# One float32 key tile becomes 16-bit for every even head, and the experts' inner values of two blocks go through one instruction with x requested four blocks ahead

## The chip, the cores and the metric

The kernel runs on one core of a Trainium2 chip. The metric is the device time in microseconds, the median of several executions. The core has five engines that run their own instruction streams and wait for one another through semaphores: TensorE (PE in the rows, with its weight loads as PEld), VectorE (DVE), ScalarE (ACT), GpSimd (POOL) and SyncE (SP), which here only issues DMAs. Matmuls write to PSUM, the other operands lie in SBUF.

## What is computed

The output of a pooled attention is the input of a routed mixture of experts (cut from the reference):

```python
# attention: q, k, v are (4, 8, 1152, 64)
q_pool = q.reshape(B, H, S // 2, 2, D).mean(axis=3)            # 576 queries per head
scores = (1.0 / np.sqrt(D)) * np.matmul(q_pool, k.transpose(0, 1, 3, 2))
attn = np.exp(scores - scores.max(-1)); attn /= attn.sum(-1) + 1e-09
x = np.matmul(attn, v)                                          # -> (4, 576, 512)
# experts: w_gate (512, 8), w_local (512, 1), w1 (8, 512, 1024), w2 (8, 1024, 512)
logits = x @ w_gate
local_gate = sigmoid(x @ w_local)
for b, s:                                                       # token by token
    fresh = argmax(logits[b, s])
    e = fresh if s == 0 or local_gate[b, s] < 0.5 else prev_e
    out[b, s] = softmax(logits[b, s])[e] * (relu(x[b, s] @ w1[e]) @ w2[e])
```

## The kernel before

**Attention** goes over 32 heads, two of which (heads n = 2p and 2p + 1, j = n % 2) are a pair p. A head has nine tiles of 128 keys, so there are 288 steps s, with n, kt = divmod(s, 9). A step emits the score matmuls of its key tile (`scores`: lines 223 and 225) and the exp of the result on ScalarE (line 227, into `PHI`, float32), one or two units that find row maxima for the head after (`max_unit`: matmuls of lines 189, 195 and 197 into one of two PSUM tiles, and a reduction on VectorE, lines 190 and 199), and, six steps late (`LAG`), the products with V (`av`). For the precision of V the kernel has two ways. A tile kt in `F32K = (4, 8)` takes float32 operands: five matmuls on `PHI` and `VX` (line 261). All other tiles take 16-bit parts: the upper half of the float32 number as bfloat16 (`top`), the rest as float16 in `PLO`, V as `VT` with a high and a low part, three matmuls (lines 263 to 265) for each of five query tiles. The rest in `PLO` is a subtraction of 576 columns (`low`, line 237), for an even step on GpSimd and for an odd one on VectorE; two steps share one call, after the exp of both. `prep_ops(p)` turns the loaded K, Q and V of a pair into operands, one op for each step from step 13 of the pair two before: among them `o6` (V to `VT`, line 159 on ScalarE, in two pieces since tile 4 is left out) and `o7` (the low part, line 162 on GpSimd, two pieces in two steps). `extra(s)` loads and splits the experts' first weights: at s = 40 + 14c VectorE runs line 510 once.

**Experts.** Tokens are sorted into 23 blocks of 128 with one expert each. Eight phases ph go over the blocks j, i = 23 ph + j: phases 0 to 3 make 256 inner values each (`mm1`, 24 matmuls of line 1061), phases 4 to 7 make 128 outputs each (`mm2`, line 1069). All engines run their streams in the order written. For a step i the loop in `experts` writes: the copy of block i + 1's weights on VectorE (line 934, three buffers `wc`); the request of x for block i + 3 (`xready`: line 988 stores x in phase 1, line 995 loads it from block 12 of phase 2 on, into six slots that are freed by twos); for the next phase's weights, 16 pieces c, a load (line 491, four buffers `wf`), three steps after it two ScalarE passes (lines 499 and 501), one step after these the low part (line 508 on GpSimd in phases 1 to 3, line 510 on VectorE else); then the block's matmuls, a relu on ScalarE (line 944) and, one step later (`pend`), the low part of the relu on VectorE (line 945). SyncE issues all these DMAs in this order, so a load that waits for its buffer holds the ones behind it.

```python
n = i + 3
if NST <= n < 4 * NST:
    xready(*divmod(n, NST))
...
f = (mm1 if ph < 4 else mm2)(i)
if pend:
    pend()
pend = f
```

Of the kernel before, what the change touches and what calls it, by code (L numbers as in the profile page):

```python
# [8 lines left out]
F32 = mybir.dt.float32  # L9
F16 = mybir.dt.float16  # L10
# [3 lines left out]
AF = mybir.ActivationFunctionType  # L14
# [11 lines left out]
F32K = (4, 8)  # L26
PREP0 = 13
# [5 lines left out]
def attention(tc, psum, stg, kT, qeo, vL, ident, emit_x, extra, load_ident, drain):  # L33
# [15 lines left out]

    VT = [lat.tile([128, 2, NKT - 2, 130], F16, name=f"vt{i}") for i in range(3)]  # L50
# [52 lines left out]
    def prep_ops(p):  # L103
# [145 lines left out]
    def av(s):  # L249
        n, kt = divmod(s, NKT)  # L250
        p, j = divmod(n, 2)
        if kt == 0:
            AV[n] = ps_a.tile([128, 512], F32, name="av", tag="av")
        a = AV[n]
        ph, pl = top(PHI[s // 2 % NPH]), PLO[s // 2 % NPH]
        v, kv = VT[p % 3], kt - (kt > F32K[0])
        for t in range(5):
            o = a[:, t * 65:t * 65 + 65]
            c = (s % 2) * Q + t * 128
            if kt in F32K:  # L260
                T.matmul(o, PHI[s // 2 % NPH][:, c:c + 128], VX[p % 2][:, j, F32K.index(kt)], start=False, stop=(kt == NKT - 1 and t == 4), skip_group_check=True)  # L261
                continue
            T.matmul(o, ph[:, c:c + 128], v[:, j, kv, 0:65], start=(kt == 0 and t == 0), stop=False, skip_group_check=True)  # L263
            T.matmul(o[:, 0:64], ph[:, c:c + 128], v[:, j, kv, 65:129], start=False, stop=False, skip_group_check=True)  # L264
            T.matmul(o, pl[:, c:c + 128], v[:, j, kv, 0:65], start=False, stop=(kt == NKT - 1 and t == 4), skip_group_check=True)  # L265
# [110 lines left out]
NST = 23  # L376
# [52 lines left out]
class Moe:  # L429
# [507 lines left out]
    def mm1(self, i, p):  # L937

        V, A = self.nc.vector, self.nc.scalar
        ph, j = divmod(i, NST)  # L940
        w = self.wcp.pop(i).rearrange("p (s k f) -> p s k f", s=2, k=4)
        x = self.xt.pop((ph, j))
        h, hl = self.hq[ph][:, 0, j], self.hq[ph][:, 1, j]
        return (lambda: self.block1(p, w, x, 0), lambda: self.block1(p, w, x, 1), lambda: A.activation(out=h, in_=p, func=AF.Relu),
                lambda: V.scalar_tensor_tensor(out=hl, in0=p, scalar=0.0, in1=h, op0=ALU.max, op1=ALU.subtract))
# [27 lines left out]
    def experts(self):  # L973
# [4 lines left out]
        nx = [NST + NST % 2]  # L978

# [18 lines left out]
        def mm1(i):  # L998
# [3 lines left out]
            f = self.mm1(i, self.ps.tile([128, 2, 128], F32, name="psh", tag="ps"))  # L1002
            for k in range(3):
                f[k]()
            return f[3]
# [14 lines left out]
        for i in range(NF, NS):  # L1020
# [11 lines left out]
            n = i + 3  # L1032
# [24 lines left out]
    def block1(self, p, w, x, ft):  # L1057
        n = 0
        for kk in range(4):
            for ws, xs_ in ((0, 0), (0, 1), (1, 0)):  # L1060
                self.nc.tensor.matmul(p[:, ft], w[:, ws, kk, ft * 128:ft * 128 + 128], x[:, 2 * kk + xs_], start=(n == 0 and ft == 0),  # L1061
# [184 lines left out]
```

## Time and profile before

| | |
|---|---|
| median of 3 runs (lowest, highest) | 759.37 us (758.96, 760.9) |
| profiled execution | 763.41 us, span of the trace 761.4 us |
| busy: PE, DVE, POOL, ACT | 697.4 us (92%), 620.5 (81%), 503.4 (66%), 477.0 (63%) |
| granted TensorE clock, mean | 0.985 of 2.4 GHz |
| DMA | 122.99 MB, mean 162 GB/s |

Busy time of matmuls is counted to their modelled ends, and they overlap, so the starts of neighbouring instructions tell more of TensorE's pace than its busy time. A wait is idle time of an engine before an instruction, with what ended it; a wait for several things is put down to the one that came last in the profile.

### The profile page before, as it was taken

Reading aid. Unit: us, or ns where it says so; the run is one execution under the profiler, and the core shown is the slowest. Engines: PE = TensorE matmul, PEld = TensorE weight load, DVE = VectorE, ACT = ScalarE, POOL = GpSimd, SP = SyncE. Lnnn points to the kernel's source line nnn. Section 1 sums busy time; section 2 is a strip of 40 time slices with the busy share of each in tenths; the row PEclk is TensorE's granted clock in tenths of the full one; section 3 lists DMA queues with packets and bytes.
Section 4 is the critical chain, followed back from the end, with each engine's and each line's share of the span. In section 5 each row is a group of like instructions: output and inputs, shape, how many; then the busy total and the mean of one; then the engine's idle time right before and its main releaser. Section 6 shows DMA issues by size and latency. Waiting matters only on the chain. (4 is left out here: it accounts for less than half of the span.)

```text
span 761.4 us, 25799 instructions
## 1 busy us (share of the span) xinstructions
PE 697.4 (92%) x10664; PEld 611.1 (80%) x10664; DVE 620.5 (81%) x1098; ACT 477.0 (63%) x971; POOL 503.4 (66%) x456
## 2 busy tenths in 40 slices
PE   3899999999999999889999998888898999999994
PEld 0487788887778877778887887888897889999994
DVE  7778888888888888888888976689889899798851
ACT  2475777677477667567766655686767675565521
POOL 6575687778367767458666435853647567777776
PEclk9999999999899999999999999999999999999998
DMA  7363643586363586354593226696828884474411
GB/s 241 97 180 121 186 119 109 160 212 154 140 187 81 166 192 169 112 174 102 153 202 72 72 31 173 219 308 214 286 93 280 279 288 165 148 230 145 127 40 32
DMA packets 90058, 122.99 MB, mean 162 GB/s; under 512 B 40552, under 2 KB 46828, under 8 KB 89936
## 3 DMA queue, kind: packets, MB, share of 16 engines
q1 hardware_dynamic: 85152, 110.41, 49.8%
q0 software_dynamic: 4784, 10.86, 4.3%
q8 instruction: 87, 1.43, 0.8%
q14 instruction: 35, 0.29, 0.1%
HBM read 79.29 MB, written 16.85 MB: 126 GB/s over the span
## 5 line engine op out<-in xcount | busy, mean ns | idle before, releaser
L227 ACT ACTIVATE ph<-sc 128x576 f32<-128x576 f32 x288 | 187.6, 652 | 118.3 <-PE sc L225 99.8
L199 DVE TENSOR_REDUCE mx<-psm 128x1 f32<-128x512 f32 (+1 forms) x300 | 193.7, 662 | 57.2 <-PE psm L197 54.9
L237 POOL TENSOR_TENSOR pl<-ph 128x576 f16<-128x576 f32 x112 | 150.2, 1342 | 43.5 <-ACT ph L227 43.5
L934 DVE COPY wc<-w 128x2048 f16 x184 | 154.4, 839 | 26.7 <-PE pso L1069 22.6
L1061 PEld LDWEIGHTS <-wc 128*128 128x128 f16 x2208 | 126.1, 98 | 20.8 <-DVE wc L934 12.1
L264 PE MATMUL av<-vt,ph 128*128 128x64 f16 x1120 | 126.9, 196 | 0.0
L263 PE MATMUL av<-vt,ph 128*128 128x65 f16 x1120 | 126.4, 193 | 0.0
L265 PE MATMUL av<-vt,pl 128*128 128x65 f16 x1120 | 126.1, 192 | 0.0
L1069 PE MATMUL pso<-wc,hq 128*128 128x128 f16 x2208 | 123.4, 219 | 0.0
L1069 PEld LDWEIGHTS <-hq 128*128 128x128 f16 x2208 | 123.3, 98 | 0.0
L264 PEld LDWEIGHTS <-ph 128*128 128x128 bf16 x1120 | 104.9, 98 | 20.1 <-issue 0.5
L1073 POOL DMA_INDIRECT out<-ob,sid x92 | 100.6, 1093 | 30.9 <-issue 18.0
L225 PE MATMUL sc<-qa,ks 65*128 65x288 f16 (+1 forms) x576 | 119.9, 290 | 0.3 <-ACT qa L213 0.3
L263 PEld LDWEIGHTS <-ph 128*128 128x128 bf16 x1120 | 106.2, 98 | 17.2 <-issue 9.6
L223 PE MATMUL sc<-qs,ks 128*128 128x288 f16 x576 | 119.7, 290 | 0.2 <-ACT ph L227 0.2
L237 DVE TENSOR_TENSOR pl<-ph 128x576 f16<-128x576 f32 x112 | 106.3, 949 | 1.9 <-ACT ph L227 1.9
L265 PEld LDWEIGHTS <-pl 128*128 128x128 f16 x1120 | 105.3, 100 | 0.0
L508 POOL TENSOR_TENSOR w<-wf,w 128x512 f16<-128x512 f32 x48 | 62.8, 1315 | 53.4 <-ACT w L501 52.9
L197 PE MATMUL psm<-ks,qs 128*128 128x512 f16 x248 | 91.1, 387 | 6.6 <-DVE mx L199 6.1
L261 PEld LDWEIGHTS av<-vx,ph 128*128 128x128 f32 x640 | 82.1, 194 | 8.6 <-issue 5.1
L1168 POOL TENSOR_TENSOR xr<-xf,xr 128x320 f16<-128x320 f32 x30 | 33.2, 1106 | 77.1 <-ACT xr L1165 77.1
L1061 PE MATMUL psh<-xr,wc 128*128 128x128 f16 x1248 | 76.1, 221 | 8.7 <-DVE wc L934 5.8
(201 smaller groups left out, 1112.5 us busy)
## 6 DMA issues: line engine op xcount, KB each, us to landing
wf<-wq SPq DMA_DIRECT2D x128, 256.0 KB
qf<-qeo SPq DMA_DIRECT2D x16, 576.0 KB
vf<-vL SPq DMA_DIRECT2D x16, 576.0 KB
ks<-kd SPq DMA_DIRECT2D x32, 288.0 KB
kf<-kT SPq DMA_DIRECT2D x15, 576.0 KB
xts<-xr SPq DMA_DIRECT2D x23, 256.0 KB
qs<-qh SPq DMA_DIRECT2D x64, 72.0 KB
ks<-kl SPq DMA_DIRECT2D x32, 144.0 KB
```

The costliest lines, as they stand in the source:

```text
L199: V.tensor_reduce(out=mx[:, i, c:c + 1], in_=m[:, 0:w], op=ALU.max, axis=AX.X)
L223: T.matmul(sc[:, c, 0:288], ksl, QS[p][:, j, c * 288:(c + 1) * 288], start=True, stop=False)
L225: T.matmul(sc[:, c, 0:288], kal, QA[p % 3][u, j, c * 288:(c + 1) * 288], start=False, stop=True)
L227: A.activation(out=PHI[g % NPH][:, r * Q:(r + 1) * Q].rearrange("p (c q) -> p c q", c=2), in_=sc[:, :, 0:288], func=AF.Exp, scale=1.0 / 16)
L237: x.tensor_tensor(out=PLO[g % NPH][:, r * Q:r * Q + Q], in0=pf, in1=top(pf), op=ALU.subtract)
L263: T.matmul(o, ph[:, c:c + 128], v[:, j, kv, 0:65], start=(kt == 0 and t == 0), stop=False, skip_group_check=True)
L264: T.matmul(o[:, 0:64], ph[:, c:c + 128], v[:, j, kv, 65:129], start=False, stop=False, skip_group_check=True)
L265: T.matmul(o, pl[:, c:c + 128], v[:, j, kv, 0:65], start=False, stop=(kt == NKT - 1 and t == 4), skip_group_check=True)
L934: self.nc.vector.tensor_copy(w, self.W[ph % 2][:, bass.ds(self.ej[j], 1), :].rearrange("p o f -> p (o f)"))
L1061: self.nc.tensor.matmul(p[:, ft], w[:, ws, kk, ft * 128:ft * 128 + 128], x[:, 2 * kk + xs_], start=(n == 0 and ft == 0), stop=(n == 11 and ...
L1069: self.nc.tensor.matmul(p, h(hs, ft), w[:, ws, ft], start=(n == 0), stop=(n == 23))
L1073: sc = self.nc.gpsimd.indirect_dma_start(out=self.out.rearrange("b s (q d) -> (b s q) d", q=4), in_=o, in_offset=None, bounds_check=NTOK * ...
```

## The change

- `FK = ((8,), (4, 8))` says which key tiles take float32 operands for j = 0 and j = 1. Tile 4 of the even heads, 16 tiles in all, takes the 16-bit way, so `low` has 16 subtractions more (step 9n + 4 is even for an even n: all on GpSimd). `VT` holds eight tiles instead of seven, `o6` becomes one ScalarE instruction of 1024 columns, and the second `o7` has 512 columns instead of 384.
- In phases 1 to 3, blocks j = 2m and 2m + 1 (up to 21) write into two halves of one PSUM tile `psh2`; the relu and its low part run once, on 512 columns, after the second: 33 instructions fewer on ScalarE and on VectorE.
- `xready` is called for block i + 4.

```diff
+FK = ((8,), (4, 8))
...
-    VT = [lat.tile([128, 2, NKT - 2, 130], F16, name=f"vt{i}") for i in range(3)]
+    VT = [lat.tile([128, 2, NKT - 1, 130], F16, name=f"vt{i}") for i in range(3)]
...
-        vk = [vf.rearrange("p h (t d) -> p h t d", d=D)[:, :, k] for k in (slice(0, 4), slice(5, 8))]
-        tk = [VT[i][:, :, k] for k in (slice(0, 4), slice(4, 7))]
+        vk = [vf.rearrange("p h (t d) -> p h t d", d=D)[:, :, k] for k in (slice(0, 4), slice(4, 8))]
+        tk = [VT[i][:, :, k] for k in (slice(0, 4), slice(4, 8))]
         def o6():
-            for x, v in zip(tk, vk):
-                A.activation(out=x[:, :, :, 0:64], in_=v, func=AF.Copy)
+            A.activation(out=VT[i][:, :, :, 0:64], in_=vf.rearrange("p h (t d) -> p h t d", d=D)[:, :, 0:8], func=AF.Copy)
...
         for r, x in enumerate((G, V)):
-            if (2 * g + r) % NKT not in F32K:
+            n, kt = divmod(2 * g + r, NKT)
+            if kt not in FK[n % 2]:
...
-            if kt in F32K:
+            if kt in FK[j]:
                 T.matmul(o, PHI[s // 2 % NPH][:, c:c + 128], VX[p % 2][:, j, F32K.index(kt)], ...
...
-    def mm1(self, i, p):
+    def mm1(self, i, p, two=None):
...
+        first = two is None or j % 2 == 0
+        go = [lambda ft=ft, p=p: self.block1(p, w, x, ft, first) for ft in range(2)]
         h, hl = self.hq[ph][:, 0, j], self.hq[ph][:, 1, j]
+        if two is not None:
+            if first:
+                return go
+            h, hl, p = self.hq[ph][:, 0, j - 1:j + 1], self.hq[ph][:, 1, j - 1:j + 1], two
...
+            if ph == 0 or j == NST - 1:
+                f = self.mm1(i, self.ps.tile([128, 2, 128], F32, name="psh", tag="ps"))
+            else:
+                if j % 2 == 0:
+                    two[0] = self.ps.tile([128, 2, 2, 128], F32, name="psh2", tag="ps")
+                f = self.mm1(i, two[0][:, j % 2], two[0])
...
-            n = i + 3
+            n = i + 4
             if NST <= n < 4 * NST:
                 xready(*divmod(n, NST))
```

Three places show what moves. On GpSimd, near the end of an even head's first half: V's low part (`vt`), the subtractions (`pl`) and the low part of finished rows (`xr`), before:

```order
L162 TENSOR_TENSOR vt_134<-vf,vt_134 128x2x4x64
L237 TENSOR_TENSOR pl_152<-ph_147 128x576
L1168 TENSOR_TENSOR xr<-xf,xr 128x5x64
L162 TENSOR_TENSOR vt_134<-vf,vt_134 128x2x3x64
L237 TENSOR_TENSOR pl_153<-ph_148 128x576
L237 TENSOR_TENSOR pl_150<-ph_145 128x576
```

and with the change:

```order
L161 TENSOR_TENSOR vt_134<-vf,vt_134 128x2x4x64
L237 TENSOR_TENSOR pl_152<-ph_147 128x576
L1180 TENSOR_TENSOR xr<-xf,xr 128x5x64
L161 TENSOR_TENSOR vt_134<-vf,vt_134 128x2x4x64
L237 TENSOR_TENSOR pl_153<-ph_148 128x576
L237 TENSOR_TENSOR pl_149<-ph_144 128x576
L237 TENSOR_TENSOR pl_150<-ph_145 128x576
```

The subtraction into `pl_149` (key tile 4) is new, between those of tiles 2 and 6, and the piece of `vt` ahead of it is a third longer.

On VectorE, the first blocks of phase 2 (`wc` is a block's weights, `hq` the inner values, ISA the read of the expert's number), before:

```order
L934 COPY wc<-w_76 128x2048
L945 SCALAR_TENSOR_TENSOR hq_10943<-psh,hq_10943 128x256
L934 ISA
L934 COPY wc<-w_76 128x2048
L945 SCALAR_TENSOR_TENSOR hq_10943<-psh,hq_10943 128x256
L934 ISA
L934 COPY wc<-w_76 128x2048
```

and with the change:

```order
L934 COPY wc<-w_76 128x2048
L951 SCALAR_TENSOR_TENSOR hq_11070<-psh_11071,hq_11070 128x512
L934 ISA
L934 COPY wc<-w_76 128x2048
L934 ISA
L934 COPY wc<-w_76 128x2048
L951 SCALAR_TENSOR_TENSOR hq_11070<-psh_11130,hq_11070 128x512
```

Only every second copy now stands behind a low part, of twice the columns.

On SyncE, from the end of phase 2 into phase 3 (x of a block into the slots `gvf`, `gkf`, `gqf`, two blocks to a slot; `wf` is a piece of weights), before:

```order
L995 DMA gvf<-xts 128x1024 x2
L995 DMA gkf<-xts 128x1024 x2
L995 DMA gqf_11710<-xts 128x1024
L491 DMA wf<-wq 128x512
L995 DMA gqf_11710<-xts 128x1024
L491 DMA wf<-wq 128x512
L995 DMA gvf<-xts 128x1024
L491 DMA wf<-wq 128x512
L995 DMA gvf<-xts 128x1024
L491 DMA wf<-wq 128x512
L995 DMA gkf<-xts 128x1024
L491 DMA wf<-wq 128x512
```

and with the change:

```order
L1002 DMA gvf<-xts 128x1024 x2
L1002 DMA gkf<-xts 128x1024 x2
L1002 DMA gqf_11773<-xts 128x1024 x2
L491 DMA wf<-wq 128x512
L1002 DMA gvf<-xts 128x1024
L491 DMA wf<-wq 128x512
L1002 DMA gvf<-xts 128x1024
L491 DMA wf<-wq 128x512
L1002 DMA gkf<-xts 128x1024
L491 DMA wf<-wq 128x512
```

Each x stands one piece of weights earlier in the queue.

## Rows read from the trace of the kernel before

**Rows 1.** Busy time of the engines in three stretches: attention, phases 1 to 3 of the experts, phases 4 to 7 (start and end in us, length, then busy us and instructions of PE, PEld, DVE, ACT and POOL, granted clock, DMA share, GB/s).

```profile
40.00:460.00 420.00, 401.11 (x5790) 335.63 (x5789) 355.52 (x650) 286.89 (x579) 281.64 (x225) 0.98 0.52 140
...
517.00:628.00 111.00, 98.66 (x1671) 94.80 (x1669) 97.93 (x155) 78.46 (x166) 62.84 (x48) 0.98 0.72 238
628.00:751.00 123.00, 123.00 (x2206) 122.96 (x2203) 93.68 (x140) 58.62 (x140) 94.90 (x87) 1.00 0.42 135
```

**Rows 2.** TensorE in order of time, two steps of a pair: start in us, duration, instruction. The first products with V are float32 (10 matmuls), the second 16-bit (15 matmuls), each followed by the next step's scores.

```profile
203.73 1.23 PE L261 MATMUL av<-vx,ph 128*128 128x65 f32 x10
204.79 0.41 PE L223 MATMUL sc<-qs,ks 128*128 128x288 f16 x2
...
205.71 0.19 PE L263 MATMUL av<-vt,ph 128*128 128x65 f16 x1
...
206.17 0.41 PE L223 MATMUL sc<-qs,ks 128*128 128x288 f16 x2
```

**Rows 3.** VectorE in order of time in one pair, around the products of the even head's tile 4 (they start at 368.7), with its idle time and what ended it in brackets.

```profile
368.69 0.69 DVE L199 TENSOR_REDUCE mx<-psm 128x1 f32<-128x512 f32 x1 [0.34 <-PE psm L197]
369.30 0.75 DVE L237 TENSOR_TENSOR pl<-ph 128x576 f16<-128x576 f32 x1
370.46 2.07 DVE L199 TENSOR_REDUCE mx<-psm 128x1 f32<-128x512 f32 x3 [0.41 <-PE psm L197]
```

**Rows 4.** TensorE in order of time, waits for VectorE's reductions: the first and last of three pairs with line 510 near those products, two steps after them; the first and last of three pairs in which a batch is routed, some four steps after them; and the second of two pairs with line 510 in step 7, in step 8.

```profile
148.60 0.38 PE L197 MATMUL psm<-ks,qs 128*128 128x512 f16 x1 [0.31 <-DVE mx L199]
346.14 0.38 PE L197 MATMUL psm<-ks,qs 128*128 128x512 f16 x1 [0.31 <-DVE mx L199]
212.00 0.38 PE L212 MATMUL psh<-ident,mn 128*65 128x128 f16 x4 [0.39 <-DVE mx L199]
432.00 0.38 PE L212 MATMUL psh<-ident,mn 128*65 128x128 f16 x4 [0.20 <-DVE mx L199]
365.95 0.38 PE L197 MATMUL psm<-ks,qs 128*128 128x512 f16 x1 [0.40 <-DVE mx L199]
```

**Rows 5.** All subtractions of line 237 by engine: shortest, median and longest in ns, first and last start.

```profile
L237 DVE TENSOR_TENSOR pl<-ph x112: 734/749/1674, 31.5 to 456.4; 128x576 f16<-128x576 f32 x112
L237 POOL TENSOR_TENSOR pl<-ph x112: 1138/1150/1837, 32.0 to 457.1; 128x576 f16<-128x576 f32 x112
```

**Rows 6.** GpSimd in order of time, the subtractions of key tiles 2 and 6 of an even head, between which the new one stands in the order.

```profile
360.96 1.66 POOL L237 TENSOR_TENSOR pl<-ph 128x576 f16<-128x576 f32 x1
363.49 1.25 POOL L237 TENSOR_TENSOR pl<-ph 128x576 f16<-128x576 f32 x1 [0.88 <-ACT ph L227]
```

**Rows 7.** VectorE in order of time at the same place: tile 5's subtraction and a piece of the experts' weights.

```profile
363.00 0.74 DVE L237 TENSOR_TENSOR pl<-ph 128x576 f16<-128x576 f32 x1
...
363.76 1.53 DVE L510 SCALAR_TENSOR_TENSOR w<-wf,w 128x512 f16<-128x512 f32 x1
```

**Rows 8.** Who waited for whom in phases 1 to 3: us in total, times, longest.

```profile
DVE hq L945 <- ACT hq L944: 11.4, 22, 2.0
...
PE psh L1061 <- DVE wc L934: 7.6, 8, 1.9
...
PE psh L1061 <- DMA gkf<-xts: 2.8, 3, 1.5
PE psh L1061 <- DMA gvf<-xts: 1.5, 3, 0.6
```

**Rows 9.** TensorE in order of time, starts of blocks in phases 2 and 3 that waited; the third is block 77.

```profile
584.06 1.50 PE L1061 MATMUL psh<-gkf,wc 128*128 128x128 f16 x24 [0.92 <-DMA gkf<-xts]
587.02 1.50 PE L1061 MATMUL psh<-gkf,wc 128*128 128x128 f16 x24 [1.46 <-DMA gkf<-xts]
...
604.77 1.50 PE L1061 MATMUL psh<-gkf,wc 128*128 128x128 f16 x24 [1.48 <-DVE wc L934]
...
622.33 2.84 PE L1061 MATMUL psh<-gkf,wc 128*128 128x128 f16 x48 [0.41 <-DMA gkf<-xts]
```

**Rows 10.** SyncE's issues in phase 3 (start, time to issue): x of block 76, a piece of weights, x of block 77, a piece, x of block 78.

```profile
596.59 0.32 SPq L995 DMA_DIRECT2D gkf<-xts  x1
599.49 0.33 SPq L491 DMA_DIRECT2D wf<-wq  x1
599.88 0.50 SPq L995 DMA_DIRECT2D gkf<-xts  x1
601.06 0.33 SPq L491 DMA_DIRECT2D wf<-wq  x1
601.49 0.39 SPq L995 DMA_DIRECT2D gqf<-xts  x1
```

**Rows 11.** VectorE in order of time in phase 2: two copies of a block's weights next to one another while GpSimd splits weights, and one with GpSimd not in its way.

```profile
569.64 1.31 DVE L934 COPY wc<-w 128x2048 f16 x1
...
571.21 1.31 DVE L934 COPY wc<-w 128x2048 f16 x1
...
577.73 0.68 DVE L934 COPY wc<-w 128x2048 f16 x1
```

**Rows 12.** The low part of the relu on VectorE in phases 1 to 3 (count, busy us, mean ns, idle before it and what ended that).

```profile
L945 DVE SCALAR_TENSOR_TENSOR hq<-psh,hq 128x256 f16<-128x256 f32 x70 | 29.2, 417 | 11.8 <-ACT hq L944 11.4
```

**Rows 13.** ScalarE in phases 1 to 3, grouped in the same way: a pass of 512 columns and the relu of 256.

```profile
L501 ACT ACTIVATE w<-wf 128x512 f16<-128x512 f32 x48 | 30.3, 630 | 1.5
...
L944 ACT ACTIVATE hq<-psh 128x256 f16<-128x256 f32 x70 | 26.0, 373 | 23.7 <-PE psh L1061 23.6
```

More of the change, by code (lines that the diff above doesn't have):

```diff
@@ L259, in av @@
             c = (s % 2) * Q + t * 128
-            if kt in F32K:
+            if kt in FK[j]:
                 T.matmul(o, PHI[s // 2 % NPH][:, c:c + 128], VX[p % 2][:, j, F32K.index(kt)], start=False, stop=(kt == NKT - 1 and t == 4), skip_group_check=True)
                 continue
-            T.matmul(o, ph[:, c:c + 128], v[:, j, kv, 0:65], start=(kt == 0 and t == 0), stop=False, skip_group_check=True)
-            T.matmul(o[:, 0:64], ph[:, c:c + 128], v[:, j, kv, 65:129], start=False, stop=False, skip_group_check=True)
-            T.matmul(o, pl[:, c:c + 128], v[:, j, kv, 0:65], start=False, stop=(kt == NKT - 1 and t == 4), skip_group_check=True)
+            T.matmul(o, ph[:, c:c + 128], v[:, j, kt, 0:65], start=(kt == 0 and t == 0), stop=False, skip_group_check=True)
+            T.matmul(o[:, 0:64], ph[:, c:c + 128], v[:, j, kt, 65:129], start=False, stop=False, skip_group_check=True)
+            T.matmul(o, pl[:, c:c + 128], v[:, j, kt, 0:65], start=False, stop=(kt == NKT - 1 and t == 4), skip_group_check=True)
         if kt == NKT - 1:
@@ L942, in mm1 @@
         x = self.xt.pop((ph, j))
+        first = two is None or j % 2 == 0
+        go = [lambda ft=ft, p=p: self.block1(p, w, x, ft, first) for ft in range(2)]
         h, hl = self.hq[ph][:, 0, j], self.hq[ph][:, 1, j]
[L944 removed]
+        if two is not None:
+            if first:
+                return go
+            h, hl, p = self.hq[ph][:, 0, j - 1:j + 1], self.hq[ph][:, 1, j - 1:j + 1], two
+        return (go[0], go[1], lambda: A.activation(out=h, in_=p, func=AF.Relu),
                 lambda: V.scalar_tensor_tensor(out=hl, in0=p, scalar=0.0, in1=h, op0=ALU.max, op1=ALU.subtract))
@@ L978, in experts @@
         nx = [NST + NST % 2]
+        two = [None]
         def transp(j):
@@ L1001, in mm1 @@
                 hq[ph] = self.hp[ph].tile([128, 2, NST, 2, 128], F16, name=f"hq{ph}", tag="s")
[L1002 to L1005, printed above, removed]
+            if ph == 0 or j == NST - 1:
[4 more added lines that the diff above has]
+                f = self.mm1(i, two[0][:, j % 2], two[0])
+            for g in f[0:3]:
+                g()
+            return f[3] if len(f) > 3 else None
         def mm2(i):
@@ L1054, in experts, with block1 @@
                 self.more = nc.values_load(self.nbi[0:1, 0:1], min_val=1, max_val=NBLK)
-    def block1(self, p, w, x, ft):
+    def block1(self, p, w, x, ft, first=True):
         n = 0
@@ L1060, in block1 @@
             for ws, xs_ in ((0, 0), (0, 1), (1, 0)):
-                self.nc.tensor.matmul(p[:, ft], w[:, ws, kk, ft * 128:ft * 128 + 128], x[:, 2 * kk + xs_], start=(n == 0 and ft == 0),
+                self.nc.tensor.matmul(p[:, ft], w[:, ws, kk, ft * 128:ft * 128 + 128], x[:, 2 * kk + xs_], start=(n == 0 and ft == 0 and first),
                                       stop=(n == 11 and ft == 1), skip_group_check=True)
```

2 lines of the change are left out of this document (1 added, 1 removed).

## The prediction

> **What bounds the kernel now.** I read the busy table by stages first, since the three parts of the change fall into two of them. In the 420 us of attention TensorE is busy for 401 us, VectorE for 356, ScalarE for 287 and GpSimd for 282; in phases 1 to 3 of the experts TensorE has 99 of 111 us; in phases 4 to 7 it has 123 of 123 [rows 1]. So nothing can be won behind 628 us, where nothing is changed either, and in the other two stages TensorE's own work and its waits are what counts. Then I read TensorE in order of time inside a pair of heads, from start to start, because busy times of overlapping matmuls say little about pace. A step with 16-bit products takes 0.46 us for them (205.71 to 206.17), a step with float32 products 1.06 us (203.73 to 204.79) [rows 2]. Third, the waits: in attention TensorE waits for VectorE's maxima now and then, some 0.3 us at a time [rows 4]; in phases 1 to 3 it waits 7.6 us for weight copies and 4.3 us for x [rows 8].
>
> **The float32 tile.** Sixteen tiles go from 1.06 to 0.46 us: 16 x 0.60 = 9.6 us less work on TensorE. The new matmuls are the same instructions on the same shapes as those of the other tiles, so the price is read, not guessed. This is the only part of which the sum is large, and the question is how much of it VectorE lets through.
>
> VectorE's reductions of row maxima are fed by TensorE through two PSUM tiles, so TensorE can be at most two units ahead. In a quiet pair VectorE is idle for 0.41 us soon after these products [rows 3], waiting for TensorE, and the second PSUM tile gives it some tenths more. If TensorE comes 0.60 us earlier, VectorE starts that much earlier and loses its idle time; I let these pairs keep the whole 0.60. In three pairs line 510 stands near the products and TensorE waits for a reduction two steps later already (148.60 to 346.14); in three others a batch is routed and it waits some four steps later (212.00 to 432.00) [rows 4]. There VectorE works without a break from before the products to the wait, so the wait only grows by what TensorE saved. I count nothing for these six. Ten pairs x 0.60 = 6.0 us.
>
> The 16 new subtractions run on GpSimd, at 1.15 us each [rows 5]: 18.4 us, and 128 more columns of V's low part per pair, at 1150/576 = 2.0 ns a column 0.26 us, 4 us in all. GpSimd has 138 us idle in attention [rows 1]; the new one falls where it stood idle for 0.88 us [rows 6], delaying tile 6's by about 0.3 us at least and 1.15 at most. The products that read it come four steps after it is issued, over 4 x 1.1 us later, so this latency is covered; if the cover went, TensorE would wait in step 10 of each pair. ScalarE's joined `o6` does one instruction more cheaply than two; it has 133 us idle [rows 1]: nothing.
>
> What is not covered is the neighbour. VectorE subtracts tile 5 at the same time, in 0.74 us next to an idle GpSimd [rows 6, 7]. Over all its subtractions the median is 0.749 us and the longest 1.674 [rows 5], so meeting a GpSimd subtraction costs between nothing and 0.92 us; I take 0.5, about the middle, since the two are issued together but GpSimd may start late. In most pairs VectorE's idle time swallows that. In two pairs line 510 follows directly, already stretched to 1.53 us [rows 7], and TensorE waits 0.40 us in step 8 [rows 4]; there it counts: 2 x 0.5 = 1.0 us. Attention: -6.0 + 1.0 = **-5.0 us**, between -9.6 (all kept, nothing met) and +5.1 (all 16 meetings at 0.92 us wait, less 9.6 kept: 14.7 - 9.6).
>
> A rule bears on this. The Trainium skill, page "SBUF — State Buffer", section "SBUF: two separate sides", says that VectorE and GpSimd share one pair of ports under an exclusive lock, and that the loser is blocked for the whole instruction. The trace agrees in kind (0.75 against 1.53 to 1.67 us for the same or similar work); by the rule each meeting could cost up to a whole GpSimd subtraction, which makes the slow rival below.
>
> **x four blocks ahead.** SyncE issues a piece of weights and then x, in program order, and pieces follow each other at 1.57 us (599.49, 601.06). x of block 77 was issued at 599.88, behind the piece of 599.49 [rows 10], and block 77 started at 604.77 [rows 9], 4.9 us later, where three blocks take about 4.0 (1.34 each by 2.84 - 1.50 in the last row of [rows 9]). Its wait of 1.48 us is put down to a copy; I count it as x's, because of those 4.9 us. All waits for x are then 2.8 + 1.5 + 1.48 = 5.8 us [rows 8, 9], in two chains: 584 to 587 us and 604 to 622 us. In the new order each x passes one piece, and so comes about 1.57 us earlier. A chain cannot shrink by more than the shift: 2 x 1.57 = 3.1 us. In the second chain the copies have a limit of their own: while GpSimd splits weights they follow at 1.57 us (569.64, 571.21), and take 1.31 instead of 0.68 us [rows 11]. I take 1.5 for the first chain and 1.0 for the second: **-2.5 us**, bounds 0 (all transfers slow down together, or slots hold them) and -5.8.
>
> The slots are freed by twos, and the first request of two now waits until block i - 1 is done, not i - 2. Behind it in SyncE's queue stands the weight piece of the same step. Where pieces wait for their own buffers (599.49, 2.6 us after x's issue was done) that is free. At the start of phase 3 buffers are empty and three pieces will go out about a block later; ScalarE needs them three steps on. I count nothing, and keep it as a rival.
>
> **Two blocks in one instruction.** 33 pairs. On VectorE two of 417 ns [rows 12] become one of 512 columns, which costs between 417 and 834 ns. ScalarE's own ratio (630 for 512 columns, 373 for 256 [rows 13]) gives 0.70 us, so 0.13 us saved each, 4.3 us in all; on ScalarE 2 x 373 - 630 = 116 ns each, 3.8 us. Little of it is on the path. Where copies are slow they alternate with GpSimd's work and the low part lies beside that [rows 11]. What can be won is in the waits of the low part for the relu (11.4 us, 22 times [rows 8]), behind which a copy stands: half of these places go. A late relu of two blocks can in turn hold one copy by the extra 0.26 us. I take **-0.5 us**, bounds -4.3 and +1.0.
>
> **Sum.** -5.0 - 2.5 - 0.5 = -8.0 us. The profiled span 761.4 becomes 753.4, the profiled execution's own 763.41 becomes 755.4. The median of the runs, 759.37, lies 4.0 below that execution; with the same difference it becomes **751.4 us**.
>
> **Rivals.** (a) *All is kept*: VectorE follows everywhere (-9.6), all waits for x go (-5.8), and late relus no longer hold copies (-2): 742, say 742 to 746.5. Against it stand the six pairs of [rows 4].
>
> (b) *VectorE becomes attention's limit*: the idle 0.41 us of [rows 3] is less than 0.60, and tile 5's subtraction takes part of the rest. If attention gives only 1 us, the time is 759.4 - 1 - 3 = 755.4, 754.5 to 757.
>
> (c) *The slots hold SyncE*: three pieces late by a block (1.3 us) at each phase's start hold ScalarE, the low part and the copies, once in phase 2 and once in phase 3: 2 x 1.3 = 2.6 lost and nothing won from x. 759.4 - 5.5 + 2.6 = 756.5, 755.5 to 758. For it speaks that ScalarE's stream is in order; against it, that the pieces have three blocks' time.
>
> (d) *Slower*: the new subtraction blocks VectorE for its whole 1.15 us, tile 5's subtraction or what follows. If VectorE has no idle time before the next wait of TensorE, the 16 cost 18.4 us against 9.6 won: +8.8, less 3 from the experts, 765. It decides from about 11 such pairs on (11 x 1.15 = 12.7, the whole gain); [rows 4] shows two.
>
> (e) *The 16-bit products of tile 4 take longer than the 1.06 us they replace*, which needs over 71 ns for each of 15. At 0.19 us, the length of one by itself [rows 2], a tile would take 2.85 us, 16 x 1.79 = +28.6, and the time would be 785 with 3 from the experts. Against it: the same 15 take 0.46 us in the rows, 31 ns each [rows 2]. A rule stands behind this rival: the Trainium skill, page "TensorE: Matmul & The Clock Gate", section "Back-to-back issue gap", gives about 81 ns for each pair of a weight load and a matmul of 128 columns in a long stream. By it an estimate is 15 x 81 = 1.2 us, which would turn the 9.6 us won into 2.2 lost; the matmuls here have 65 columns, and the measurement decides.
>
> **Chances and range.** Forecast 0.61 (747 to 754.5), (a) 0.09, (b) 0.13, (c) 0.10, (d) 0.06, (e) 0.01. 0.3% of 759.4 is 2.3 us, about what a measurement of this kernel can tell from no change: faster is below 757.1, slower above 761.7. Faster: 0.61 + 0.09 + 0.13 + half of (c), less a little, 0.87; same: the other half of (c) and (e), 0.07; slower: (d), 0.06. The range reaches into (b) and (c) above and to (a) below: 746.5 to 757.5, which leaves out (a), (d) and parts of (c) and the forecast's edges.
>
> **What would show it.** In the profile after: TensorE from tile 4's first product to the next scores 0.46 us in even heads; attention's end 4 to 6 us earlier; waits for L199's maxima grown in the six pairs by up to 0.6 us; VectorE's subtraction of tile 5 above 1 us; x issued before the piece of its step and waits for x halved; the low part at about 0.70 us, 33 times. Wrong would be: attention's end hardly earlier (b), or later (d); ScalarE waiting more for weights at phase 3's start (c).

## Result, and the profile after

The changed kernel takes **770.12 us** (median of 4 runs, 768.83 to 772.47) where the kernel before took 760.13 beside it (4 runs, 758.96 to 763.59): ratio 1.0114, 95% interval 1.0078 to 1.0149. It is slower; 751.4 us was forecast. In all ratios here, runs more than 1.5% above the shortest run of the same kernel are left out, which takes three of the six of e18. The profiled execution took 770.49 us, span 768.7 (before 761.4).

The gain of the float32 tile is there. TensorE in order of time at the place of [rows 2], tile 4 of an even head: its last 16-bit product and the next scores (the first product starts at 203.87, so 0.47 us for the tile, 1.06 before).

```profile
203.87 0.19 PE L263 MATMUL av<-vt,ph 128*128 128x65 f16 x1
...
204.34 0.41 PE L222 MATMUL sc<-qs,ks 128*128 128x288 f16 x2
```

What answers to [rows 1], in its columns, attention and phases 1 to 3:

```profile
40.00:464.00 424.00, 395.93 (x5882) 326.74 (x5880) 371.14 (x650) 286.51 (x564) 308.10 (x241) 0.98 0.51 137
526.00:636.00 110.00, 98.61 (x1663) 94.39 (x1661) 83.77 (x121) 76.16 (x132) 66.69 (x48) 0.98 0.73 241
```

TensorE has 5 us less work in attention, VectorE 15.6 us more for the same 650 instructions. Line 237 shows where (as [rows 5]: shortest, median, longest): VectorE's median rises from 749 to 964 ns. The subtraction of tile 5, which stands beside the new one, goes from about 0.74 us to between 1.25 and 1.63 in ten of the 16 pairs.

```profile
L237 POOL TENSOR_TENSOR pl<-ph x128: 1136/1162/1841, 29.7 to 459.2; 128x576 f16<-128x576 f32 x128
L237 DVE TENSOR_TENSOR pl<-ph x112: 734/964/1949, 26.9 to 458.7; 128x576 f16<-128x576 f32 x112
```

TensorE's waits that answer to [rows 4] (0.31, 0.31 and 0.40 us before); one in a pair that was counted as keeping its gain; and one in the routed pair of [rows 4]'s 212.00, two steps after the products, where there was no wait before:

```profile
147.00 0.38 PE L196 MATMUL psm<-ks,qs 128*128 128x512 f16 x1 [0.91 <-DVE mx L198]
345.41 0.38 PE L196 MATMUL psm<-ks,qs 128*128 128x512 f16 x1 [0.92 <-DVE mx L198]
366.47 0.38 PE L196 MATMUL psm<-ks,qs 128*128 128x512 f16 x1 [1.25 <-DVE mx L198]
126.97 0.38 PE L196 MATMUL psm<-ks,qs 128*128 128x512 f16 x1 [0.70 <-DVE mx L198]
205.42 0.38 PE L196 MATMUL psm<-ks,qs 128*128 128x512 f16 x1 [0.43 <-DVE mx L198]
```

Behind attention, TensorE waits for the transposes of the last batch (line 540), which it did not before, and the granted clock is half (1.2 of 2.4 GHz, "half clock" from here on) in the stretch after it. TensorE in order of time; the transposes (count, shortest, median and longest time that SyncE took to issue one, in ns, first and last start); and the stretch, in the columns of [rows 1]:

```profile
465.66 0.81 PE L567 MATMUL psg<-wgh,xT 128*128 128x9 f16 x26 [1.66 <-DMA xT<-xr]
```

```profile
L540 SPq DMA_TRANSPOSE xT<-xr x5: 1244/1279/2647, 454.3 to 459.6; - x5
```

```profile
467.60:474.40 6.80, 6.09 (x67) 5.34 (x65) 3.58 (x14) 3.00 (x6) 1.17 (x2) 0.50 0.74 258
```

The same two views of before, where the longest of these times was 1.9 us and the clock was full:

```profile
L540 SPq DMA_TRANSPOSE xT<-xr x5: 1244/1283/1908, 451.6 to 457.5; - x5
```

```profile
462.00:475.00 13.00, 10.67 (x204) 9.58 (x201) 10.63 (x48) 7.54 (x12) 5.70 (x10) 1.00 0.60 191
```

Who waited for whom in phases 1 to 3 (as [rows 8]); the low part of two blocks follows (as [rows 12]):

```profile
DVE hq L951 <- ACT hq L950: 22.0, 20, 1.9
...
ACT wf L499 <- DMA wf<-wq: 11.3, 15, 2.3
PE psh L1073 <- DVE wc L934: 9.3, 13, 1.9
...
PE psh L1073 <- DMA gkf<-xts: 1.2, 1, 1.2
```

ScalarE's waits for weights (line 499) before, in the same stretch:

```profile
ACT wf L499 <- DMA wf<-wq: 7.7, 10, 1.9
```

The low part of two blocks:

```profile
L951 DVE SCALAR_TENSOR_TENSOR hq<-psh,hq 128x512 f16<-128x512 f32 x33 | 22.7, 686 | 22.0 <-ACT hq L950 22.0
```

The 7.3 us of span, from the starts of the same instructions in both traces: start of attention -2.6; attention +4.7; from its last product with V to block 23 +5.3; phases 1 to 3 -0.6; rest +0.5.

### The profile page after: what moved, and what is told of

It reads as the page before. It is cut to its first block, busy times and chain, and to the rows that moved or that the text cites. A ratio compares the mean times of both kernels' runs of the same rounds, so it can differ in the third digit from the quotient of the medians.

```text
span 768.7 us, 25922 instructions
## 1 busy us (share of the span) xinstructions
PE 690.7 (90%) x10744; PEld 603.3 (78%) x10744; DVE 625.5 (81%) x1065; ACT 475.3 (62%) x922; POOL 532.6 (69%) x472
## 4 chain that ended last, share of the span: by engine, by line
PE 48%; DVE 23%; DMA 12%; issue 6%; ACT 5%; POOL 4%; SPq 1%; POOLq 0%; DVEq 0%; ACTq 0%
PE pso L1081 8%; DVE mx L198 7%; PE sc L222 6%; PE sc L224 6%; DMA wf<-wq 6%; PE psm L196 6%; DVE pl L237 5%; PE av L261 4%; DMA out<-ob,sid 4%; PE psh L1073 4%; PE av L264 3%; PE av L265 3%; PE av L263 3%; DVE w L510 3%; POOL out L1085 2%
## 5 line engine op out<-in xcount | busy, mean ns | idle before, releaser
L237 POOL TENSOR_TENSOR pl<-ph 128x576 f16<-128x576 f32 x128 | 176.3, 1385 | 23.9 <-ACT ph L226 23.9
L934 DVE COPY wc<-w 128x2048 f16 x184 | 140.1, 773 | 28.6 <-PE pso L1081 21.8
L264 PE MATMUL av<-vt,ph 128*128 128x64 f16 x1200 | 137.3, 196 | 0.0
L263 PE MATMUL av<-vt,ph 128*128 128x65 f16 x1200 | 136.9, 194 | 0.0
L265 PE MATMUL av<-vt,pl 128*128 128x65 f16 x1200 | 136.4, 193 | 0.0
L263 PEld LDWEIGHTS <-ph 128*128 128x128 bf16 x1200 | 114.5, 98 | 27.2 <-issue 19.4
L264 PEld LDWEIGHTS <-ph 128*128 128x128 bf16 x1200 | 113.3, 98 | 22.5 <-issue 1.7
L237 DVE TENSOR_TENSOR pl<-ph 128x576 f16<-128x576 f32 x112 | 125.8, 1123 | 1.5 <-ACT ph L226 1.5
L265 PEld LDWEIGHTS <-pl 128*128 128x128 f16 x1200 | 113.7, 100 | 0.0
L501 ACT ACTIVATE w<-wf 128x512 f16<-128x512 f32 x128 | 80.0, 627 | 5.7 <-DMA wf<-wq 4.0
L1180 POOL TENSOR_TENSOR xr<-xf,xr 128x320 f16<-128x320 f32 x30 | 28.9, 965 | 73.5 <-PE sc L224 67.6
```

The costliest lines, as they stand in the source:

```text
L263: T.matmul(o, ph[:, c:c + 128], v[:, j, kt, 0:65], start=(kt == 0 and t == 0), stop=False, skip_group_check=True)
L264: T.matmul(o[:, 0:64], ph[:, c:c + 128], v[:, j, kt, 65:129], start=False, stop=False, skip_group_check=True)
L265: T.matmul(o, pl[:, c:c + 128], v[:, j, kt, 0:65], start=False, stop=(kt == NKT - 1 and t == 4), skip_group_check=True)
L934: self.nc.vector.tensor_copy(w, self.W[ph % 2][:, bass.ds(self.ej[j], 1), :].rearrange("p o f -> p (o f)"))
```

## Experiments

For each run the table gives, worked out from its trace: attention (first score to last product with V) and how much of that the clock was at half; the stretch from there to block 23; phases 1 to 3; and the mean change of a pair of heads against before, over those of the pairs 1 to 14 that have no half clock in either trace (their number; these are the quiet pairs). Nearly all of them repeat to 0.02 us where the attention code is the same, as e3, e12 and e13 show, so this column is the sharpest. The exceptions are 0.34 us in pair 11 (e2 and e11 against before, e15 against e9), 0.14 in pair 13 (e15 against e9) and 0.99 in pair 9 (e1 against the changed kernel and e8). The pairs differ much among themselves, so two means over different pairs are not quite comparable.

| run | attention (at half clock) | to block 23 | phases 1-3 | per quiet pair | time, ratio to before |
|---|---|---|---|---|---|
| before | 437.2 (13.7) | 55.5 | 110.4 | | |
| after | 441.9 (23.9) | 60.7 | 109.8 | +0.22 (9) | 1.0114 [1.0078, 1.0149] |
| e1_keys | 441.3 (23.9) | 62.0* | 109.8 | +0.15 (10) | 1.0022* [0.9976, 1.0069] |
| e2_pair | 440.0 (23.9) | 61.4* | 107.2 | -0.03 (11) | 1.0049* [1.0003, 1.0094] |
| e3_ahead | 438.1 (13.7) | 63.1* | 107.4 | 0.00 (11) | 0.9987* [0.9952, 1.0021] |
| e4_nosub | 441.8 (23.9) | 63.3* | 107.2 | +0.15 (8) | 1.0006* [0.9969, 1.0042] |
| e5_vprep | 443.4 (20.5) | 57.1 | 108.0 | +0.31 (8) | 1.0051 [1.0014, 1.0087] |
| e6_o6two | 438.8 (23.9) | 59.9 | 105.2 | -0.07 (9) | 1.0011 [0.9964, 1.0058] |
| e7_after_o6two | 435.0 (10.2) | 59.6 | 109.7 | -0.07 (9) | 1.0050 [1.0016, 1.0083] |
| e8_after | 439.7 (17.1) | 61.5 | 109.2 | +0.25 (10) | 1.0042 [1.0003, 1.0081] |
| e9_keep | 434.6 (10.2) | 55.8 | 108.4 | -0.01 (10) | 0.9985 [0.9955, 1.0014] |
| e10_last | 443.7 (27.3) | 56.6 | 108.1 | +0.16 (10) | 1.0066 [1.0035, 1.0096] |
| e11_pair | 437.0 (13.7) | 57.4 | 108.1 | -0.03 (11) | 1.0035 [0.9998, 1.0072] |
| e12_ahead | 438.3 (17.1) | 57.4 | 106.7 | -0.01 (10) | 1.0029 [0.9996, 1.0062] |
| e13_both | 437.2 (13.7) | 55.8 | 109.3 | 0.00 (11) | 0.9996 [0.9965, 1.0028] |
| e14_select | 438.0 (17.1) | 56.2 | 110.6 | -0.08 (10) | 0.9984 [0.9956, 1.0012] |
| e15_keep_ahead | 439.2 (27.3) | 55.7 | 108.6 | -0.07 (9) | 0.9983 [0.9959, 1.0008] |
| e16_move510 | 435.5 (17.1) | 56.8 | 107.6 | -0.11 (10) | one run |
| e17_three_m1 | 434.6 (17.1) | 55.0 | 109.2 | -0.26 (10) | 0.9967 [0.9942, 0.9992] |
| e18_all_quiet | 435.1 (34.1) | 56.5 | 109.8 | -1.01 (8) | 0.9843 [0.9778, 0.9907] |

*The first four ran on a chip on which the kernel before takes 797.8 us: quiet pairs are as elsewhere, but from block 92 to the end 160 to 163 us pass instead of 134 to 136. Their times say little, their attention much.

**e1, the key-tile part alone.** Tile 4 of the even heads in 16-bit parts with all that belongs to it, the experts as before.

> The key-tile part alone (tile 4 of the even heads in 16-bit parts, with its 16 subtractions, the joined o6 and the longer o7), nothing changed in the experts. If this part is what makes the changed kernel slower, it takes 767 to 772 us by itself, with attention 3 to 6 us longer than before and the stretch from attention's end to block 23 longer too. If the fault lies in the experts' parts, it takes 750 to 756 us.

Attention took 441.3 us: the loss there comes from this part. The time could not tell on that chip.

**e2, e3, the experts' parts alone.**

> The pairing of two blocks in one relu and one low part alone. The prediction's step says -0.5 us (758.5 to 759.5). A rival read from the trace of the changed kernel: the low part's waits for the late relu of two blocks (22 us there, 11 before) hold the copies behind them, then 1 to 3 us slower, 761 to 763.

> The request of x four blocks ahead alone. The prediction's step says -2.5 us (757). If the copies of weights are the limit right behind x in phases 2 and 3, x's waits go and the copies' waits grow by as much: within 1 us of before.

Neither touches attention, and in phases 1 to 3 both lie among the kernels with the experts unchanged (105.2 to 110.6). They were run again as e11 and e12.

**e4, without the new subtractions.** This tells the lock theory (rival d) from the others. The kernel leaves out the rest of tile 4's numbers and reads their upper half twice. The edit against e1:

```diff
-            if kt not in FK[n % 2]:
+            if kt not in F32K:
...
-            T.matmul(o, pl[:, c:c + 128], v[:, j, kt, 0:65], ...
+            T.matmul(o, (ph if kt == 4 else pl)[:, c:c + 128], v[:, j, kt, 0:65], ...
```

> The key-tile part without its 16 new subtractions: for tile 4 of the even heads the third product reads the upper half a second time in place of the rest, so part of the computation is left out; everything else, with the joined o6 and the longer o7, is as in the key-tile part alone. If the price of the subtractions (VectorE held by GpSimd) is what takes the gain back, attention is 6 to 9 us shorter than before, 750 to 754 us. If VectorE's maxima give the pace in any case, attention gains at most 2 us, 757 to 760. If the longer o6 and o7 and what they shift are at fault, attention is as long as before or longer, 760 to 768.

Attention is as long as with them (441.8 against 441.3). So neither the new subtractions nor their meetings are the main cause. They do cost something, in few places: step 8 of the pairs 5 and 12 grows by 0.84 us with them and 0.20 without, step 6 of pair 15 by 0.74 and 0.00.

**e5, V's preparation alone.** The products and subtractions are those of before. In place of e1's `FK`:

```diff
+FK = ((4, 8), (4, 8))
```

> Only V's preparation in the new form: eight tiles in VT, o6 in one instruction, the second o7 on 512 columns. The products stay as before (tile 4 in float32 for both heads), and there are no new subtractions. If the delay that the joined o6 gives to GpSimd and so to the later subtractions is what costs the time, attention (first score to last product with V; 437.2 us before) is 5 to 9 us longer, 442 to 446. If the new subtractions or the quicker products are the cause, it stays at 437 within 0.5 us.

Attention is 6.2 us longer, a quiet pair 0.31 us, with no gain anywhere to set against it: this is the main cause of what attention lost. The trace shows how, in pair 4, which starts at 130.79 us before and at 130.74 here. All engines in order of time, of which the rows are ScalarE's `vt`, GpSimd's two pieces of `o7`, VectorE's subtraction and the reduction behind it, and TensorE's next unit. Before:

```profile
133.21 1.03 ACT L159 ACTIVATE vt<-vf 128x512 f16<-128x512 f32 x2
133.91 1.13 POOL L162 TENSOR_TENSOR vt<-vf,vt 128x512 f16<-128x512 f32 x1 [0.50 <-ACT vt L159]
...
137.38 0.88 POOL L162 TENSOR_TENSOR vt<-vf,vt 128x384 f16<-128x384 f32 x1
...
138.08 0.80 DVE L237 TENSOR_TENSOR pl<-ph 128x576 f16<-128x576 f32 x1
138.80 0.68 DVE L199 TENSOR_REDUCE mx<-psm 128x1 f32<-128x512 f32 x1
...
139.78 0.22 PE L195 MATMUL psm<-kd,qd 128*128 128x128 f16 x1
```

With V's preparation in the new form:

```profile
133.15 1.05 ACT L159 ACTIVATE vt<-vf 128x1024 f16<-128x1024 f32 x1
...
134.28 1.13 POOL L162 TENSOR_TENSOR vt<-vf,vt 128x512 f16<-128x512 f32 x1 [0.92 <-ACT vt L159]
...
137.74 1.11 POOL L162 TENSOR_TENSOR vt<-vf,vt 128x512 f16<-128x512 f32 x1
137.75 1.71 DVE L238 TENSOR_TENSOR pl<-ph 128x576 f16<-128x576 f32 x1
...
139.38 0.68 DVE L199 TENSOR_REDUCE mx<-psm 128x1 f32<-128x512 f32 x1
...
140.12 0.22 PE L195 MATMUL psm<-kd,qd 128*128 128x128 f16 x1 [0.27 <-DVE mx L199]
```

The two ScalarE instructions of before, with 512 and 384 columns, take 1.03 us together, and the one of 1024 columns 1.05 (two of 512 take 1.14 in e6). But GpSimd could start behind the first of the two, and now waits 0.92 us instead of 0.50. Its next work in this half of the pair comes 0.4 to 0.9 us later. VectorE's subtraction, which took 0.80 us when GpSimd's piece ended 0.18 us into it, now begins beside a piece of 1.11 us and takes 1.71; the maxima are late, and TensorE waits. The Trainium skill, page "SBUF — State Buffer", section "SBUF: two separate sides", says that of the two engines the one that starts first has the shared ports for its whole instruction. This trace agrees: VectorE starts 0.01 us behind GpSimd and takes 0.91 us longer.

Over all of VectorE's subtractions the median goes from 749 to 908 ns in e5:

```profile
L238 DVE TENSOR_TENSOR pl<-ph x112: 734/908/1744, 26.8 to 460.0; 128x576 f16<-128x576 f32 x112
```

**e6, o6 in two pieces; e7, the same in the whole change; e8, the change again.** The edit of e6 and e7:

```diff
         def o6():
-            A.activation(out=VT[i][:, :, :, 0:64], in_=vf.rearrange(...)[:, :, 0:8], func=AF.Copy)
+            for x, v in zip(tk, vk):
+                A.activation(out=x[:, :, :, 0:64], in_=v, func=AF.Copy)
```

> The key-tile part alone, but with o6 in two pieces of 512 columns, so that the first o7 can start behind the first piece, as before; the new subtractions, the products and the longer second o7 as in the change. If the joined o6 is the cause, attention takes 432 to 436 us (before 437.2, the key-tile part with the joined o6 441.3). If the longer o7 or the new subtractions are, it stays at 440 to 442.

> The whole change, but with o6 in two pieces. If the joined o6 is the cause, it is 5 to 9 us faster than the changed kernel of the same call, so about 2 to 5 us faster than before; if not, it equals the changed kernel.

> The changed kernel again, beside the others on one chip: 10 us (1.1%) slower than before, with attention at 441 to 442 us and, where the cover of the last batch's transposes is lost, 1.7 us of waiting of TensorE for them behind attention's end.

The same attention code took 438.8 us in e6 and 435.0 in e7, with 23.9 and 10.2 us at half clock: 13.7 us of half clock go with 3.8 us. So e6 lies between its two ranges and e7 in the first. Two comparisons are free of this. At the same 23.9 us of half clock, e1 and the changed kernel, with one piece, take 441.3 and 441.9 us, e6 with two 438.8: 2.5 and 3.1 us. And in the eight pairs that are quiet in both e6 and e8, one piece costs 0.28 us on average (0.39 to 0.42 in six, 0.12 in one, and 0.35 less in one). So the joined `o6` costs attention some 3 us. In e6 VectorE's median of line 237 is 1.02 us, longer than in the changed kernel: not the length of the subtractions tells the loss, but whether TensorE waits behind them.

The times of e7 and e8 do not resolve this (765.53 and 766.68, where 5 to 9 us were expected). The changed kernel was slower again, by 0.4% this time and not the expected 1.1%, with 439.7 us of attention (441 to 442 expected) and 0.94 us of waiting for the transposes (1.7 expected).

**e9 and e10, the last pair.** e9 leaves head 30 as it was; e10 changes only head 30 (both with `o6` in two pieces).

```diff
+FK = lambda n: F32K if n % 2 or n == 30 else (8,)      # e9
+FK = lambda n: (8,) if n == 30 else F32K               # e10
```

> The key-tile part alone with o6 in two pieces, and head 30 (the even head of the last pair) keeping its float32 tile 4. If the 0.6 us that this one head saves is what uncovers the last batch's transposes, TensorE does not wait for them, keeps its full clock behind attention, and the stretch from the last product with V to block 23 is 55 to 57.5 us (before 55.5; with the change in all heads 59.6 to 61.5); time 757 to 761 where before takes 760 to 762. If that stretch is longer for another reason (V's preparation, the clock), it stays at 59 or more.

> The opposite: only head 30 takes its tile 4 in 16-bit parts, all others as before (V's preparation with eight tiles, o6 in two pieces). If the lost cover is the cause, TensorE waits 0.9 to 1.7 us for the transposes, runs at half clock for some us after it, and the stretch to block 23 is 59 to 61.5 us; time 3 to 5 us over before. If not, 55 to 57.5 us and within 1 us of before. Attention also tells what the longer second o7 costs by itself: 437.2 us if nothing.

e9 came out as expected: no wait for the transposes, 55.8 us to block 23, and 1.1 us below before. e10 did not: no wait either. The transposes of e7 (which waits 1.25 us) and of e10 (shortest, median and longest time to issue one of the five), and those of e1 with TensorE's wait for them:

```profile
L542 SPq DMA_TRANSPOSE xT<-xr x5: 1243/1287/2592, 450.3 to 455.5; - x5
```

```profile
L542 SPq DMA_TRANSPOSE xT<-xr x5: 1245/1288/1677, 459.0 to 464.7; - x5
```

```profile
L541 SPq DMA_TRANSPOSE xT<-xr x5: 1243/1286/2512, 453.1 to 458.4; - x5
```

```profile
463.82 0.31 PE L568 MATMUL psg<-wgh,xT 128*128 128x9 f16 x6 [0.43 <-DMA xT<-xr]
```

The 0.6 us less cover is in e7 and e10 (the first transpose starts 9.6 us before the last product's end, 10.2 before the change), and by itself it makes no wait, as e10 shows. In e7, as in e6, e8 and the changed kernel, the fifth transpose also takes 1.2 to 1.4 us longer to issue than the median. In e1 it does so with the cover of before (10.2 us), and TensorE still waits 0.43 us. So the late fifth transpose makes the wait, and the lost cover lengthens it. It stands in the six traces in which all 16 tiles take the 16-bit way, and in none of the other 14; why stays open.

e10 also carries the price of the longer second pieces of `o6` and `o7` by themselves, +0.16 us in a quiet pair. That is an estimated 2.6 of the 6.5 us by which its attention is longer; the rest goes with 27.3 us at half clock against 13.7.

**e11, e12, e13, the experts' parts again, apart and together.**

> The pairing of two blocks in one relu and one low part alone, once more beside undisturbed runs. The prediction's step says -0.5 us. The earlier run (0.5% slower, 0.0 to 0.9%) says +4: then the waits of the low part for the late relu hold the copies, and TensorE waits for copies 2 us or more longer in phases 1 to 3.

> The request of x four blocks ahead alone, once more. The prediction's step says -2.5 us. If weight copies are the next limit, it is 0 to -1 us: TensorE's waits for x go (5.8 us before) and those for copies grow by most of it.

> Only the two changes in the experts, together (pairing and x four blocks ahead); attention as before. The prediction's steps say -3.0 us. In the profiles each alone leaves phases 1 to 3 (block 23 to 92) at 106.7 to 108.1 us, where kernels with the experts as before show 105.2 to 110.4 (mean 108.1) and the three with the whole change 109.2 to 109.8. If the two hurt each other (x in time, but the late relu of two blocks holds the copies), phases 1 to 3 take 109 to 110 us, TensorE's waits for copies 9 to 10 us, and the time is 2 to 4 us over before; if not, 106 to 108 us and the time within 1 us of before or below.

TensorE's and VectorE's waits in phases 1 to 3 (us in total, times, longest), e12 and then e13:

```profile
DVE hq L945 <- ACT hq L944: 8.7, 21, 1.2
PE psh L1061 <- DVE wc L934: 7.5, 10, 1.4
```

```profile
DVE hq L951 <- ACT hq L950: 19.6, 19, 2.5
...
PE psh L1073 <- DVE wc L934: 9.4, 11, 1.9
```

With x four ahead no wait for x is left in either trace, and copies are what TensorE waits for: 7.5 us in e12, where the kernel before has 7.6 and 4.3 for x on top. With the pairing too, VectorE waits 19.6 us for late relus and TensorE 9.4 for copies, and the stretch is 109.3 us, as expected for two changes that hurt each other, but kernels with the experts unchanged reach 110.6 as well. The time does not follow: 0.9996. No gain of 3 us is there, and no loss either that these runs can measure. The pairing alone came out 0.35% slower in e11 and 0.49% in e2, at the edge of what they can tell, and TensorE waited no longer for copies in e11 (5.6 us) than before, where 2 us more were expected.

**e14, e15, what may be kept.** e14 changes only the pairs in which the runs had shown a gain, V's preparation too; e15 is e9 with x four ahead.

```diff
+QP = (0, 1, 2, 13)
+FK = lambda n: (8,) if n % 2 == 0 and n // 2 in QP else F32K
```

> Tile 4 of the even heads in 16-bit parts only in the pairs 0, 1, 2 and 13, in which the runs so far show that the 0.6 us is kept; V's preparation of eight tiles (o6 in two pieces) in these alone, everything else as before. If the price of V's preparation and the lost 0.6 in the other pairs are what eats the gain, attention is 1.5 to 2.5 us shorter than before at the same time at half clock, and the time 1 to 2.5 us below before; if the half clock decides, anything from -2 to +3 us.

> The key-tile part with o6 in two pieces and head 30 left as before, and x four blocks ahead, without the pairing. If x ahead gives the 0.7 us that phases 1 to 3 show without the pairing, it is 1 to 2 us below before (the kernel without x ahead was 1.1 us below); if x ahead costs what its own timing shows (+0.3%), 1 to 2 us above.

Both about 0.2% faster, within what can be told from nothing. e14's attention, expected 1.5 to 2.5 us shorter, is 0.8 us longer, with 3.4 us more at half clock.

**e16, e17, e18, VectorE's line 510 moved.** All are e9 with pieces of the experts' weights split at another step of attention.

```diff
-                if r == 10:
+                if r == 10 and c not in (3, 8, 12):
                     m.w_lo(0, c, wt.pop(c), "V")
+            if s in (88, 158, 214):                        # e16; e17: s in (91, 163, 217)
+                m.w_lo(0, (s - 46) // 14, wt.pop((s - 46) // 14), "V")
```

```diff
+            c = min(15, (s - 40) // 14)                    # e18
+            if c in wt and s == min(x for x in range(40 + 14 * c, 300) if x % 18 in (1, 15)):
+                m.w_lo(0, c, wt.pop(c), "V")
```

> The key-tile part with o6 in two pieces and head 30 left as before, with VectorE's line 510 of the pairs 4, 8 and 11 moved six steps later. If VectorE, kept busy by line 510, takes back the 0.6 us in these pairs, step 12 of each takes 1.17 us, where it took 1.64, 1.42 and 1.64 us before and 2.25, 1.74 and 2.25 with the quick products. If something else limits there, step 12 keeps the 1.74 to 2.25 us.

> The key-tile part with o6 in two pieces and head 30 left as before, and VectorE's line 510 of the pairs 4, 8 and 11 moved into step 1 of the next pair, where VectorE is idle for 0.65 us in step 1 and 0.9 us in step 2. If VectorE's idle time is what decides, step 12 of these pairs takes 1.17 us as in the run that moved line 510 six steps, and the next pairs 5, 9 and 12 do not grow by the 1.05 us they grew by there: 1 to 1.5 us less in each of the three, 758 to 760 us where before takes 762 to 763. If line 510 costs the same wherever it stands, the three pairs and those behind them come out as without the move and the time stays at 0.9985 of before.

> The same with all sixteen of line 510 moved to the next step 1 or step 15 of a pair, the steps in which VectorE is idle for 0.6 to 0.9 us in pairs without a routed batch. By the idle time of VectorE up to 3 us below the kernel with three moved; where a batch is routed step 15 is full and some of it is lost, so between 755 and 761 us.

TensorE in order of time in step 12 of pair 4, from scores to the next scores, in e9 and then e16:

```profile
146.00 0.41 PE L224 MATMUL sc<-qs,ks 128*128 128x288 f16 x2
...
147.57 0.38 PE L198 MATMUL psm<-ks,qs 128*128 128x512 f16 x1 [0.92 <-DVE mx L200]
148.25 0.41 PE L224 MATMUL sc<-qs,ks 128*128 128x288 f16 x2
```

```profile
142.69 0.41 PE L224 MATMUL sc<-qs,ks 128*128 128x288 f16 x2
...
143.85 0.28 PE L224 MATMUL sc<-qs,ks 128*128 128x288 f16 x1
```

2.25 us become 1.16, and in the pairs 8 and 11 too (1.74 and 2.25 to 1.17). But the pairs behind 4 and 11 grow by 0.8 us over e9. In e17 they grow by 0.36 instead, and the three gain 0.9 to 1.1; e17 is the first that is faster beyond its interval. With all sixteen pieces moved a quiet pair is 1.0 us shorter than before: six runs between 744.0 and 763.5 us, median 755.9, against 763.0 (17 runs). Four of the six are below the shortest of the 17 (758.3). **e18 is very likely faster than both kernels**; by how much, six runs that scatter over 19 us do not say. Line 510 moved without the quick products was not run.

## Why the prediction was wrong

**The float32 tile, the failed step.** "ScalarE's joined `o6` does one instruction more cheaply than two; it has 133 us idle [rows 1]: nothing", and the longer `o7` counted as hidden in GpSimd's idle time. The first looked at the engine that does the work and not at the one that waits for its first half. The two together are an estimated 16 x 0.31 = 5 us by e5, about half of it the longer second pieces (16 x 0.16 by e10); beside the quick products the joined `o6` alone costs some 3 us (e6 against e1 and the changed kernel). This alone turns -5.0 into nothing.

Its other terms, one by one. 16 x 0.60 = 9.6 us: right, step 10 lost 0.60 us in all 16 pairs (1.77 to 1.17, in the last 1.55 to 0.95). Six pairs that lose it: right in the pairs and the size (step 12 of the pairs 4, 6, 8, 10, 11 and 14, in 8 together with step 11, grows by 0.6), and e16 shows in three that VectorE's line 510 is why. In the three with a routed batch (6, 10, 14) the loss is a new wait of 0.43 us at that place, not the growth of the wait that [rows 4] shows further on. But the pairs 3 and 7 lose it too (steps 16 and 15), so 4.8 us were kept and not 6.0. The quiet 0.41 us of [rows 3] were no safe sign. The new subtraction's meetings: they lengthen tile 5's subtraction as forecast, and the two pairs named are the right ones, at about 0.64 us each and not 0.5; but pair 15 adds 0.9: 2.2 us, not 1.0. Sum: -4.8 + 2.2 + 5 = +2.4, where attention showed +4.7 and, run again, +2.5. The first has 10.2 us more at half clock than the kernel before, the second 3.4; by e6 and e7 (3.8 us for 13.7) that is an estimated 2.8 and 0.9 us of it, which leaves 1.9 and 1.6 for the code.

**Behind attention: no step at all.** The prediction looked for cover of the new subtraction and of x, not for what the last pair's own products cover. The fifth transpose took 1.4 us longer to issue than the median, the 0.6 us saved in head 30 took away cover, TensorE waited 1.66 us, and half clock followed: +5.3 us. e9 shows that leaving this one head alone takes the wait away. That the wait brings the half clock is not shown: the four kernels that wait 0.9 us or more have 6.8 us of it right there, but e12, e14 and e16 have 3.4 at the same place without a wait.

**x four ahead, -2.5.** The first half is right: x is issued earlier and its waits went, from 4.3 to 1.2 us, and to none in e12. The gain did not follow: e12's time leaves no room for it (1.0029, from 0.9996 on), e3's would (0.9987, from 0.9952 on), e13's shows none. The waits for copies grew with the pairing beside it (9.3 and 9.4 us) and not without (7.5 against 7.6), so that the copies take it back is shown only for the two changes together.

**Two blocks, -0.5.** 33 low parts at 686 ns (0.70 said). "Half of these places go" is wrong: 22 waits for the relu became 20, and 11.4 us became 22.0. Alone the pairing gave no gain in either run (e2, e11).

**The rivals.** (d) gave 765 by a lock on the new subtractions in 11 pairs or more; e4 says that this is not what happened, though the lock is at work elsewhere. (b), VectorE as the limit, holds for eight pairs of 16. Of (c) one sign is there, ScalarE's waits for weights, which grew from 7.7 to 11.3 us, but x's waits went all the same, and TensorE's waits for x and copies fell from 11.9 to 10.5 us. (a), all kept, and (e), slower products, did not occur (0.47 us a tile).

## What to carry to other kernels

Where two instructions become one, look at who starts on the first half: the merged one costs the waiting engine its head start, even where the engine that runs it is idle. Where VectorE and GpSimd both work from SBUF, a shift of 0.4 us changes the meetings behind it (e5), so price the shift over the whole period and not the new instruction alone. Before speeding up the tail of a stage, list what that tail covers; and when a faster engine only waits longer, move the limiting engine's optional work into its idle steps: on top of the quick products that gave the only gains beyond their intervals here (e17, e18).

## What was not expected of the hardware

Kernels with unchanged attention repeat a quiet pair to 0.02 us, on different chips too (but for one pair, 0.34 us shorter in two of them right behind a stretch of half clock). What differs most between executions is the half clock: 10 to 34 us of attention, in pair 10 in all 20 traces, in pair 6 in 16, and at other places in each kernel; the one shown above fell right behind the wait of 1.66 us. Over five sets of 17 to 35 runs of the kernel before, 0.01 less of mean granted clock went with 3.6 to 7.3 us more. So differences of 3 us need many runs, or pairs without half clock.

On one chip all kernels lost some 27 us in phases 4 to 7. In 11.7 us of that stretch TensorE stood idle for nothing that the profile shows; the rest is not explained. The idle time in e3 (us in total, times, longest), which the kernel before does not have in [rows 1]'s last stretch on its own chip:

```profile
PE pso L1069 <- issue: 11.7, 31, 1.0
```
